# Cosine of the first four pairs of chunks from a quarter turn that TensorE adds to the phases in place

## The chip, the cores and the metric

One core of a Trainium2 chip runs the whole problem in one launch. The metric is the device time in microseconds. Five engines of the core work side by side, each through its own queue in order: TensorE (PE, matmuls into PSUM), VectorE (DVE), ScalarE (ACT, activation functions by table), GpSimd (POOL) and SyncE (SP), which here only issues DMAs. In the profile PEld is TensorE's weight load.

## The reference, cut to what matters

A gated linear recurrence with a complex decay is run over 768 steps for 4 batches and 8 heads of 48 channels; its output, with the heads put side by side (384 channels), goes through a normalised two-layer block with a residual:

```python
mag = np.sqrt(a_re * a_re + a_im * a_im)
scale = np.minimum(mag, 0.999) / (mag + 1e-06)
a_re_n, a_im_n = (a_re * scale, a_im * scale)
for t in range(S):                       # S = 768
    ar, ai = a_re_n[:, :, t, :, None], a_im_n[:, :, t, :, None]
    new_re = ar * S_re - ai * S_im
    new_im = ar * S_im + ai * S_re
    kv = np.einsum('bhd,bhe->bhde', k[:, :, t], v[:, :, t])
    S_re, S_im = (new_re + kv, new_im)
    y[:, :, t] = np.einsum('bhd,bhde->bhe', q[:, :, t], S_re)
...
xn = (x - mu) / np.sqrt(var + 1e-06) * g_ln          # x is y, heads side by side
ch = np.maximum(xn @ w_ch1, 0.0) @ w_ch2             # 384 -> 1536 -> 384
return x + ch
```

## The kernel before, in words

The recurrence is done in chunks of 128 steps. With `l` the running sum of the logarithm of the decay's size and `phi` the running sum of its angle, a product of decays between two steps is `exp(l_t - l_s) * cos(phi_t - phi_s)`, and the cosine of a difference splits into products of cosines and sines. So each key is multiplied by `exp(-l)` and stacked as (cos, sin) copies, each query by `exp(l)` and stacked likewise, and a chunk becomes ordinary masked attention plus a carried state `G`.

Two chunks make a *pair* `P`, twelve pairs in all, three to a batch. Pair 0 is worked in two halves of four heads (`PARTS = {0: 2}`). A step's name carries the pair, the half and sometimes a part: `sin.0.1` is the sine of the second half of pair 0, `mm1.2.0.1` the first layer of pair 2, column group 0, second part. Steps numbered by chunk (`atm.5`, `x.5`, `y.5`) belong to pair 5 // 2. The steps of a pair, with the engine by the letter after the colon in the plan (P, A, V, G, S for PE, ACT, DVE, POOL, SP):

- `are`, `aim`, `q`, `k`, `vf`: loads. `ln`, `iv` (ACT): logarithm and inverse of the real part. `r`: the ratio of imaginary to real part. `r2`, `u`, `l`: half the logarithm of 1 + r², added to the first logarithm, then capped, which gives the log of the decay's size. `th` (ACT): arctangent of `r`.
- `dec` (PE, L459): running sums of `l` by triangular matmuls into PSUM; `e`, `en` (ACT, L463): exponentials of them. `dps`, `decc`: the decay over a whole pair.
- `ph` (PE, L474 and L477): running sums of the angle in turns, into PSUM, with the carry of the pair before and an offset of 192 put in by the matrix `pick`. With that offset the low 16 bits of each float are the fraction of a turn, so that a 16-bit integer view `v16` of the bank is the angle reduced to (-half, half) turn. `car` (ACT L486 or DVE L489): the carry to the next pair.
- `sin` (ACT, L502): sine of `v16`. `abs` (ACT L496 or DVE L498): its absolute value into the tile `sh`. `cos` (ACT, L505): sine of a quarter turn less `sh`.
- `ke`, `qe`, `ks`, `qs`: multiplication of keys and queries by `en`, `e`, cosine (part 0) and sine (part 1). `kT`, `qT` (PE transposes, L561) with the copies `ksT`, `qsT` out of PSUM, or a DMA transpose issued by SP (L566) in their place.
- `am` (PE, L584), `atm` (DVE, times the mask), `gm`, `G` (state), `y` (PE), `x` (copy of the chunk's output), `bn` and `rstd` (mean and variance, inverse root; POOL L670 and L672), `xtr`, `xT` (transpose).
- `mm1` (PE, L684): first layer; `relu`; `mm2` (PE, L705): second layer; `ot` (DVE L719) or `oa` and `ot` (ACT L710, POOL L717): scale by `rstd` and add `x`; `st`: store.

Beside the pairs: the two weight matrices come in by `wl.0` (`w1b`) and `wl.1` (`w2b`), DMAs that POOL issues. Before each stands a one-element copy, `gate.0` and `gate.1`, which waits for a load (`k.0.1`, `aim.1.0`) so that the weights do not go ahead of it. `wgc`, `wp.*` (PE) and nine `wc.*` (DVE, L371) fold the layer's gain and mean into `w1b`. `warm.*` are matmuls without use that fill PE while it has nothing to do. `tab.log` and `tab.trig` (L739) load ACT's table for logarithm and exponential, or for sine and arctangent.

All order is written out by hand. `PLAN` is a list of steps; `Graph.run` goes through it and emits each step on the engine and PSUM bank that stand behind its name, so each engine's queue is the plan's order cut down to that engine. Tiles turn in rings (`RINGS`), PSUM has eight banks. A step that waits holds up everything behind it on its engine. The plan opens so:

```
are.0.1:S tab.log.0:A ln.0.1:A iv.0.1:A aim.0.1:S are.0.0:S pad.ks.1:G one:G ue:G car0.1:G cmean:G pick:G
ident:G uth:V zdec:G r.0.1:G aim.0.0:S are.1.0:S ln.0.0:A iv.0.0:A r.0.0:V gln:S aim.1.0:S k.0.0:S are.3.0:S
k.0.1:S r2.0.1:A u.0.1:A pad.ks.2:G l.0.1:V ln.1.0:A r2.0.0:G gate.1:G q.0.0:S q.0.1:S warm.0:P1 warm.1:P1
```

Of the kernel before, what the change touches and what calls it, by code (L numbers as in the profile page):

```python
# [33 lines left out]
GATES = (("k", 0, 1), ("aim", 1, 0))  # L34
# [17 lines left out]
warm.60:P4 warm.61:P4 ph.1.0:P2 k.1.1:S qe.0.1.0:V cos.0.1:A qs.0.1.0:V cos.0.0:A dec.0.0:P1 sin.0.0:A0
aim.3.0:S vf.1.1:S k.1.0:S abs.1.0:V2 car.1.0:V2 vf.1.0:S q.1.1:S ks.0.1.0:G pad.qs.1:G mask:G tab.log.1:A
en.0.0:A1 e.0.0:A1 qs.0.1.1:V ke.0.0.0:V qe.0.0.0:V ks.0.0.0:V ks.0.0.1:V warm.62:P5 warm.63:P5 warm.64:P5
warm.65:P5 warm.66:P5 warm.67:P5 warm.68:P5 warm.69:P5 warm.70:P5 warm.71:P5 warm.72:P5 warm.73:P5
warm.74:P5 warm.75:P5 warm.76:P5 warm.77:P5 warm.78:P5 warm.79:P5 warm.80:P5 warm.81:P5 warm.82:P5 kT.1:P4
k.2.0:S wl.0:G qs.0.0.1:V u.1.0:A ln.2.0:A qs.0.0.0:V dps.0:P5 k.2.1:S iv.2.0:A l.1.0:V kT.0:P6 qT.1:P7
tab.trig.1:A cos.1.0:A v.0:A ksT.0:V6 r.2.0:G ksT.1:V4 decc.0:V5 wgc:V qsT.1:V7 qT.0:P0 gm.0:P1 dec.1.0:P4
am.1:P6 th.2.0:A sin.1.0:A2 tab.log.2:A e.1.0:A4 r2.2.0:G u.2.0:A pad.qs.2:G qsT.0:V0 am.0:P2 G.0:V1
atm.1:V6 atm.0:V2 y.1:P0 y.0:P6 ln.3.0:A iv.3.0:A wp.2:P7 qe.1.0.0:G x.0:A6 l.2.0:V dec.2.0:P2 wl.1:G  # L60
en.1.0:A4 wp.0:P6 e.2.0:A2 x.1:A0 wc.2.0:V7 wc.2.2:V7 en.2.0:A2 are.4.0:S xtr.0:P0 wc.2.1:V7 dps.1:P7
xtr.1:P4 r.3.0:G xT.0:A0 wp.1:P5 decc.1:A7 ph.2.0:P2 wc.0.0:V6 wc.0.1:V6 bn.0:V wc.0.2:V6 r2.3.0:A xT.1:A4
wc.1.2:V5 wc.1.1:V5 wc.1.0:V5 ke.1.0.0:G ke.1.0.1:G ks.1.0.0:G v.1:G qe.1.0.1:G mm1.0.2.1:P6 gm.1:P1 G.1:V1
# [24 lines left out]
k.6.0:S qsT.9:S relu.3.1:V2 qe.5.0.1:V qs.5.0.0:V rstd.3:G q.6.1:S aim.8.0:S st.5:S mm1.3.2.0:P6 qT.8:P5
mm1.3.2.1:P6 ln.7.0:A gm.9:P1 relu.3.2:A6 vf.5.0:S mm2.7.0:P4 dec.6.0:P2 qs.5.0.1:G qsT.8:V5 mm2.7.1:P4
# [112 lines left out]
def kernel(  # L202
# [568 lines left out]
```

## Time and profile before

| | us |
|---|---|
| median of five runs | 197.81 (196.57 to 198.13) |
| the profiled execution, its own time | 196.92 |
| its span, first to last instruction | 195.0 |
| first `mm1` matmul starts | 37.70 |
| last `mm2` group starts | 187.25, and 24 matmuls follow each other |
| last `ot` | 191.35, 0.62 long |

The granted TensorE clock was 1.00 in every stage. The page gives busy time, share and count of instructions of each engine; a group line gives source line, engine, operation, what it writes and reads, how often, busy us and mean ns. In the stage table each line is a stretch of 10 us with the busy us of PE, PEld, DVE, ACT and POOL, then clock, share of the DMA engines, and GB/s. The chain of waits is followed back from the last instruction and shows, piece by piece, start, length and the work that the rest waited for.

### The profile page before, as it was taken

How to read it: one execution, taken by the hardware profiler on the slowest of the kernel's cores; microseconds unless marked ns; L12 is line 12 of the kernel's file. 1: busy time of each engine (PE TensorE's matmuls, PEld its weight loads, DVE VectorE, ACT ScalarE, POOL GpSimd, SP SyncE). 2: the span in 40 equal slices, each digit the busy share in tenths (PEclk: the TensorE clock that was granted, in tenths of full speed). 3: DMA queues.
4: the chain of work that ended last, by engine and by line, in shares of the span. 5: the costliest groups of instructions: out<-in, count | busy, mean ns of one | idle time of the engine just before them, and what ended most of it. 6: DMA issues, size and time to landing. Idle time of an engine off the chain costs nothing.

```text
span 195.0 us, 5114 instructions
## 1 busy us (share of the span) xinstructions
PE 174.1 (89%) x2031; PEld 133.4 (68%) x2032; DVE 159.9 (82%) x268; ACT 164.0 (84%) x226; POOL 108.2 (55%) x127
## 2 busy tenths in 40 slices
PE   4987455899999999999999997999999999899992
PEld 3775433577687676697887785786877758687771
DVE  1459999999999999999998799699969969835702
ACT  4799995999899999999999998997979989465160
POOL 8545558715939258045949699234981486430230
PEclk9999999999999999999999999999999999999999
DMA  5999999999998399899799989998998999992322
GB/s 150 241 237 257 175 243 179 186 243 181 227 262 190 78 187 250 202 250 241 143 237 215 218 136 285 174 221 210 256 200 152 155 197 123 266 212 88 113 84 82
DMA packets 132936, 37.76 MB, mean 194 GB/s; under 512 B 127920, under 2 KB 132528, under 8 KB 132912
## 3 DMA queue, kind: packets, MB, share of 16 engines
q1 hardware_dynamic: 130960, 35.07, 85.8%
q0 software_dynamic: 1952, 2.36, 7.5%
q8 instruction: 16, 0.26, 0.5%
q14 instruction: 8, 0.07, 0.1%
HBM read 28.31 MB, written 4.72 MB: 169 GB/s over the span
## 4 chain that ended last, share of the span: by engine, by line
PE 43%; DVE 22%; DMA 11%; ACT 10%; issue 6%; SPq 4%; POOL 2%; DVEq 0%; POOLq 0%
PE banks L705 16%; PE banks L684 12%; DMA are<-in_a_re_dram 4%; DVE atm L280 4%; SPq L566 3%; DVE w1b L371 3%; DVE l L449 3%; DMA qsT<-qs 2%; DVE h L697 2%; PE banks L584 2%; PE banks L561 2%; DMA out_dram<-ot 2%; DMA q<-in_q_dram 2%; ACT L739 2%; PE banks L459 2%
## 5 line engine op out<-in xcount | busy, mean ns | idle before, releaser
L705 PE MATMUL banks<-w2b,h 128*128 128x384 bf16 x288 | 55.5, 326 | 1.2 <-DVE atm L280 1.1
L684 PE MATMUL banks<-xT,w1b 128*128 128x256 bf16 x432 | 52.4, 272 | 0.7 <-ACT xT L275 0.4
L684 PEld LDWEIGHTS <-w1b 128*128 128x128 bf16 x432 | 41.3, 98 | 7.6 <-issue 1.7
L705 PEld LDWEIGHTS <-h 128*128 128x128 bf16 x288 | 26.2, 97 | 14.9 <-issue 1.6
L280 DVE TENSOR_TENSOR atm<-banks,mask 128x1024 bf16<-128x1024 f32 x24 | 28.9, 1216 | 4.5 <-PE banks L584 4.2
L695 ACT ACTIVATE h<-banks 128x1024 bf16<-128x1024 f32 x27 | 27.0, 1022 | 5.1 <-PE banks L684 4.9
L739 ACT ACT_TABLE_LOAD x20 | 25.7, 1283 | 1.1 <-PEq L755 0.8
L280 POOL TENSOR_TENSOR ks<-ke,trig 128x768 bf16<-128x768 bf16 (+1 forms) x11 | 17.9, 1634 | 12.3 <-DVE ke L280 7.4
L280 POOL TENSOR_TENSOR qe<-q,e 128x384 bf16<-128x384 f32 x16 | 15.9, 1003 | 13.5 <-ACT e L463 10.1
L280 POOL TENSOR_TENSOR r<-aim,are 128x768 f16<-128x768 f32 (+1 forms) x9 | 16.7, 1854 | 10.6 <-ACT are L433 10.6
L280 POOL TENSOR_TENSOR ke<-k,en 128x384 bf16<-128x384 f32 x17 | 17.1, 1012 | 8.2 <-ACT en L463 8.1
L719 DVE SCALAR_TENSOR_TENSOR ot<-banks,rstd,x 128x384 f32<-128x384 f32 x20 | 12.0, 609 | 8.4 <-PE banks L705 6.0
L584 PE MATMUL banks<-qsT,ksT 128*128 128x128 bf16 x192 | 14.6, 219 | 2.2 <-DVE qsT L277 1.6
L584 PEld LDWEIGHTS <-ksT 128*128 128x128 bf16 x192 | 12.2, 98 | 4.6 <-issue 3.0
L734 PE MATMUL banks<-u_e 128*128 128x256 f16 x83 | 11.9, 310 | 2.8 <-POOL u_e L312 2.8
L670 POOL TENSOR_SCALAR rstd<-mv 128x2 f32<-128x2 f32 x12 | 2.8, 236 | 19.8 <-DVE mv L648 19.1
L634 PE MATMUL banks<-v,atm 128*128 128x48 bf16 x192 | 11.9, 183 | 2.1 <-DVE atm L280 2.0
L449 DVE SCALAR_TENSOR_TENSOR l<-r,w 128x768 f16<-128x768 f16 (+1 forms) x13 | 12.9, 990 | 0.9 <-ACT r L445 0.8
L647 DVE BATCH_NORM_STATS2 stats<-x 128x6 f32<-128x384 bf16 x24 | 13.2, 548 | 0.3 <-ACT x L275 0.3
L634 PEld LDWEIGHTS <-atm 128*128 128x128 bf16 x192 | 10.5, 96 | 4.2 <-DVE atm L280 3.2
L280 DVE TENSOR_TENSOR qs<-qe,trig 128x768 bf16<-128x768 bf16 (+1 forms) x21 | 12.1, 597 | 1.1 <-POOL qe L280 0.8
L431 ACT ACTIVATE w<-are 128x768 f32<-128x768 f32 (+1 forms) x13 | 10.3, 793 | 2.8 <-DMA are<-in_a_re_dram 2.8
(91 smaller groups left out, 379.0 us busy)
## 6 DMA issues: line engine op xcount, KB each, us to landing
k<-in_k_dram SPq DMA_DIRECT2D x24, 192.0 KB, 3.8
q<-in_q_dram SPq DMA_DIRECT2D x24, 192.0 KB, 4.1
vf<-in_v_dram SPq DMA_DIRECT2D x24, 192.0 KB, 4.1
out_dram<-ot SPq DMA_DIRECT2D x24, 192.0 KB, 3.3
are<-in_a_re_dram SPq DMA_DIRECT2D x11, 384.0 KB, 4.8
aim<-in_a_im_dram SPq DMA_DIRECT2D x11, 384.0 KB, 5.4
w1b<-in_moe_w_ch_dram POOLq DMA_DIRECT2D x1, 1152.0 KB, 9.6
w2b<-in_moe_w_ch_dram POOLq DMA_DIRECT2D x1, 1152.0 KB, 12.9
```

Of the source, the lines that this page charges most:

```text
L280: {"DVE": nc.vector, "POOL": nc.gpsimd}[eng(name)].tensor_tensor(**kw)
L431: add(f"ln.{X}", lambda S_=S_: act(out=S_("w"), in_=S_("are"), func=AF.Ln), needs=[f"are.{X}"], uses=[("are", P), ("w", P)])
L449: nc.vector.scalar_tensor_tensor(out=S_("l"), in0=S_("r2"), scalar=0.5, in1=S_("w"), op0=ALU.mult, op1=ALU.add)
L584: nc.tensor.matmul(ps[:, h], lhsT=T("ksT", n)[:, h], rhs=T("qsT", n)[:, h], start=True, stop=True)
L634: nc.tensor.matmul(ps[:, h], lhsT=T("atm", n)[:, h], rhs=T("v", P)[:, c, h], start=True, stop=nfirst)
L647: nc.vector.bn_stats(out=T("stats", n), in_=T("x", n))
L684: nc.tensor.matmul(ps[:, jj], lhsT=w1b[:, dc, ts(gi * JG + jj, C)], rhs=T("xT", P)[:, dc].rearrange("p c t -> p (c t)"), start=(dc == 0), ...
L695: act(out=dst, in_=src, func=AF.Relu)
L705: nc.tensor.matmul(bank(f"o.{n}")[:, 0:DM], lhsT=T("h", P)[:, j, ts(c, C)], rhs=w2b[:, j], start=(j == 0), stop=(j == NJ - 1))
L719: nc.vector.scalar_tensor_tensor(out=T("ot", n), in0=bank(f"o.{n}")[:, 0:DM], scalar=T("rstd", P)[:, ds(c, 1)], in1=T("x", n), op0=ALU.mul ...
L734: g.add(f"warm.{i}", lambda i=i: nc.tensor.matmul(bank(f"warm.{i}")[:, 0:256], lhsT=u_e[:, 0, 0], rhs=u_e[:, 1].rearrange("p j t -> p (j t ...
L739: g.add(f"tab.{nm}.{i}", lambda tab=tab: nc.scalar.preload_act_table_set(tab))
```

## The change

For pairs 0 to 3 the `abs` steps are gone. After `sin` and `car` have read the phases, PE adds 0.25 (a quarter turn) to the same PSUM bank by one-row matmuls (`qt`, with the row of `pick` that holds ones), and `cos` is a second sine of the same view. Pairs 4 to 11 keep `abs`. Because `qt` adds to a bank that is already summed, `ph` sets its start flag once for a bank.

With it come: `rstd` may run on ACT, as a logarithm and an exponential (eight of twelve do); `wgc` may run on ACT and does; the cap of `l` is a step of its own, `lc`; both gates are gone, so that `wl.0` and `wl.1` go out where they stand in POOL's order; and the plan is a new one throughout. 142 steps change their engine and nearly all their place. The number of steps by engine that differ most (before, after): `ot` on DVE 20, 14 and on POOL 4, 10; `oa` on ACT 4, 10; `relu` on ACT 27, 24 and on DVE 9, 12; `x` on ACT 17, 10 and on DVE 7, 14; `ks` on POOL 11, 7; `qs` on POOL 5, 8; table loads 20, 23; `kT` and `qT` on PE 23, 22; `warm` 83, 98. The lines of the after kernel lie further down by 4 to 24: `cos` from `qt` is L513, `relu` on ACT L719, `mm1` L708, `mm2` L729, the table loads L763.

```diff
-GATES = (("k", 0, 1), ("aim", 1, 0))
+QUARTER = {0, 1, 2, 3}
...
+    eps_b = pool.tile([C, 1], FP32, name="eps_b")
+    qrow = pool.tile([C, DM], FP16, name="qrow")
...
+    g.add("qrow", lambda: nc.gpsimd.memset(qrow[ds(HALF, 1)], 0.25))
...
-    for i, (nm, P, c) in enumerate(GATES):
-        g.add(f"gate.{i}", lambda nm=nm, P=P, c=c: nc.gpsimd.tensor_copy(
...
     g.add("wl.0", lambda: nc.gpsimd.dma_start(
-        out=w1b, in_=moe_w_ch1.rearrange("(dc p) j -> p dc j", p=C)), needs=["gate.0"])
+        out=w1b, in_=moe_w_ch1.rearrange("(dc p) j -> p dc j", p=C)))
...
                     nc.tensor.matmul(ps[:, c], lhsT=pick[rows], rhs=T("car", P)[rows, fs],
-                                     start=True, stop=False)
+                                     start=(c == 0 or NS == 1), stop=False,
+                                     skip_group_check=True)
...
+            if P in QUARTER:
+                def f_qt(X=X, view=view):
+                    ps = view(f"ph.{X}")
+                    for c in range(R):
+                        nc.tensor.matmul(ps[:, c], lhsT=pick[ds(HALF, 1)], rhs=qrow[ds(HALF, 1), 0:W],
+                                         start=False, stop=True, skip_group_check=True)
+                add(f"qt.{X}", f_qt, needs=[f"ph.{X}", f"sin.{X}", "qrow"]
+                    + ([] if last else [f"car.{X}"]), ps=(f"ph.{X}", nb))
+                add(f"cos.{X}", lambda fs=fs, v16=v16: act(
+                    out=T("trig", P)[:, 0, :, fs], in_=v16(), func=AF.Sin, scale=TWO_PI_SAFE / TURN),
+                    needs=[f"qt.{X}"], uses=[("trig", P)], ps=(f"ph.{X}", nb))
+            else:
...
+            if eng(f"rstd.{P}") == "ACT":
+                act(out=t, in_=T("mv", P)[:, :, 1], func=AF.Ln, bias=eps_b)
+                act(out=t, in_=t, func=AF.Exp, scale=-0.5)
+                return
```

The new plan opens so (the `warm` steps that follow are left out):

```
are.0.0:S tab.log.0:A ln.0.0:A iv.0.0:A are.0.1:S one:G ln.0.1:A iv.0.1:A are.1.0:S aim.0.1:S car0.1:G
pad.qs.2:G aim.0.0:S k.0.0:S aim.1.0:S are.2.0:S q.0.0:S k.1.0:S aim.2.0:S zdec:G mask:G gln:S q.0.1:S
pad.ks.1:G ident:G pick:G ue:G car0.0:G pad.qs.0:G uth:V k.0.1:S vf.0.1:S pad.ks.0:G r.0.0:V ln.1.0:A
iv.1.0:A tab.trig.0:A th.0.0:A r.0.1:G th.0.1:A
...
ph.0.1:P0 vf.0.0:S r2.0.0:G r2.0.1:V r.1.0:V cmean:G r2.1.0:V
are.3.0:S q.1.1:S k.1.1:S aim.3.0:S tab.log.1:A u.0.0:A l.0.0:V lc.0.0:V car.0.1:A0 u.0.1:A u.1.0:A l.0.1:V
...
ln.2.0:A e.0.1:A1 iv.2.0:A dec.0.0:P2 e.0.0:A2
...
dps.0:P3 en.0.0:A2 en.0.1:A1 ph.0.0:P2 l.1.0:V lc.1.0:V r.2.0:V
k.2.0:S vf.1.0:S car.0.0:V2 tab.trig.1:A sin.0.0:A2 dec.1.0:P4 sin.0.1:A0 decc.0:A3 qrow:G
```

And where `qt` stands among PE's steps and ACT's in pairs 2 and 3:

```
mm1.0.2.0:P6 mm1.0.2.1:P6 qs.1.0.0:V qs.1.0.1:V relu.0.2:A6 mm1.0.0.1:P4 mm1.0.0.0:P4 relu.0.0:A4
ksT.2:A3 qt.2.0:P0 ph.3.0:P6 qe.2.0.0:V car.3.0:V6 cos.2.0:A0 l.3.0:V mm1.0.1.0:P4 mm1.0.1.1:P4 qT.3:P2
qT.2:P3 sin.3.0:A6 qsT.3:V2 qsT.2:V3 relu.0.1:A4 gm.2:P0 qt.3.0:P6 am.3:P4 G.2:A0 lc.3.0:V cos.3.0:A6
```

## The prediction

> **What bounds the kernel now.** I read the page first, then the stage table, then the chain of waits in order of time. The page:
>
> ```profile
> span 195.0 us, 5114 instructions
> PE 174.1 (89%) x2031; PEld 133.4 (68%) x2032; DVE 159.9 (82%) x268; ACT 164.0 (84%) x226; POOL 108.2 (55%) x127
> PE 43%; DVE 22%; DMA 11%; ACT 10%; issue 6%; SPq 4%; POOL 2%; DVEq 0%; POOLq 0%
> L739 ACT ACT_TABLE_LOAD x20 | 25.7, 1283 | 1.1 <-PEq L755 0.8
> ```
>
> Three engines are above 80%, so the share says little; the stages say more (columns: stage, then busy us of PE, PEld, DVE, ACT, POOL):
>
> ```profile
> 20.00:30.00 10.00, 5.31 (x92) 4.14 (x92) 9.87 (x19) 9.88 (x12) 6.08 (x5) 1.00 1.08 214
> 30.00:40.00 10.00, 7.06 (x73) 4.44 (x75) 9.93 (x16) 7.62 (x14) 7.47 (x6) 1.00 1.21 183
> 60.00:70.00 10.00, 9.46 (x119) 6.88 (x118) 9.80 (x16) 9.81 (x17) 5.68 (x5) 1.00 0.59 117
> 90.00:100.00 10.00, 10.00 (x137) 8.05 (x136) 9.97 (x17) 9.92 (x15) 7.56 (x6) 1.00 0.92 205
> 140.00:150.00 10.00, 10.00 (x133) 7.71 (x131) 7.87 (x16) 8.56 (x13) 6.01 (x6) 1.00 0.88 184
> ```
>
> From 20 to 100 us DVE and ACT are full; afterwards PE alone is. The chain of waits (start, length, what) agrees, and gives PE's pace when nothing delays it:
>
> ```profile
> 36.80 2.63 DVE w1b L371 x4
> ...
> 80.41 1.30 PE banks L705 x8
> ...
> 82.36 0.65 PE banks L459 x4
> ...
> 84.03 1.31 PE banks L684 x12
> ...
> 90.14 0.45 PE banks L584 x8
> ...
> 90.75 0.33 PE banks L477 x2
> ```
>
> So `mm2` costs PE 0.163 us a matmul, `mm1` 0.109, a transpose or an `am` product 0.056, a 384-column f16 matmul 0.163. Summed over the plan, without the fillers called `warm`, PE has 156.9 us of work. I call time minus PE work done so far the lag. From the starts in the timeline: the first `mm1` starts at 37.7 with 11.3 done (lag 26.4); `mm1.0.0.0` at 40.9 (26.8, after `w1b` on DVE); `mm1.3.0.0` at 81.6 (30.4); `mm1.4.0.0` at 100.1 (30.9); `mm1.8.0.0` at 148.1 (32.5); the last `mm2` ends at about 191.2 (34.3), and 3.8 us of `ot` and store follow. Hence 195.0 = 156.9 + 34.3 + 3.8. The profiled run took 196.92, so 1.9 lies around the span; the median of the five runs, 197.81, is 0.9 above it.
>
> **Part 1, the quarter turn.** Five `abs` go: on ACT 0.49 + 2 x 0.81 (L496), on DVE 0.56 + 0.95 (L498). Five `cos` read PSUM instead of `sh`: priced like `sin` (L502, 806 against 932; half size 484 against 604), 0.6 less. Together ACT -2.7, DVE -1.5. Added are ten `qt` matmuls of one row and 384 or 192 columns. No such shape is in the trace; the nearest is L474 (96 rows, 384 columns, 327 ns alone, 0.163 in a row), the floor 0.056 of a transpose. I take the pace of L474: 1.3 us; ends 0.6 and 2.8. Each `qt` also makes PE wait for `sin` and `car`. Behind `qt.1.0` on PE stand `y.1` and the `wp` products, which wait for `atm.1` (30 us) anyhow; behind `qt.2.0` stand `ph.3.0` and `mm1.0.1`; behind `qt.3.0` stand `am.3` and `mm2.0.0`. I walk `sin.2.0` to its end at 40.4 and `mm1.0.0.0` to 40, so no stall, and `sin.3.0` to 44.9 where PE is free at 44; if that cover is gone each costs up to 1 us.
>
> **Part 2, the new order moves work between engines.** Count of steps times the mean of the row (ns: `relu` 1022 on ACT, 1212 on DVE; `x` 478, 551; `G` 484, 548; copies of `ksT`/`qsT` 1025, 683; `ot` 609 on DVE, 915 on POOL; `qs` and `ks` 1940 and 1706 on POOL, about 600 on DVE; `r2` 844 on ACT, 1468 on POOL; `rstd` 947). ACT: abs and cos -2.7; three other abs moved, net +0.8; three more table loads 3 x 1.283 = +3.9; eight `rstd` from POOL, two tiny activations each, nearest rows 0.16 (48x8 copy) and 0.48 (128x384), taken at 0.2 by size, +3.2 (2.6 to 7.7); six `oa` (586 ns) +3.5; `qsT` and `ksT` copies +2.0; `wgc` +0.8 and `v` +0.8; less three `relu` -3.1, seven `x` -3.4, `r2` -1.3, `G`, `xT` and `decc` -2.3. Sum +2.2. DVE: abs -2.5; `relu` +3.6, `x` +3.9, `G` +1.6, `ks` and `qs` +0.6, `xT` and `decc` +1.0; `ot` -3.7, `ksT` and `qsT` -2.0, `wgc` and `v` -1.4. Sum +1.1. POOL: `ot` +5.5, `qs` +5.8, `r2` +2.9, `ks` -6.8, `rstd` -7.6, gates -0.4. Sum -0.6. PE: `qt` +1.3, transposes -0.3, sum +1.0, so 157.9. Nothing is saved in sum; what can change the time is when the work is due. DMA transposes stay 27.
>
> The Trainium skill ("ScalarE: Activation LUTs", section on table sets) says to batch activations by set, which speaks against 23 loads instead of 20. Its terms price a load at about 2.7 us; by that the three loads would be 8.1, but the rows here show 1283 ns twenty times. The same page ("What ACT_TABLE_LOAD costs") puts an activation with a pointer bias at 280 ns and one without at 186 ns plus 0.833 ns an element; by that eight `rstd` are an estimated 3.8, which no run here shows yet.
>
> **Part 3, the opening (0 to 41 us).** Today half 1 of pair 0 gets its decay first and its angles after; now the angles of both halves come first (trig table), then the decays. I walk it by the rows of today's opening. SP issues the loads 0.5 us apart and they arrive at some 200 KB a us, so `are.0.0` is there at 3.4 as now, `are.1.0` at 5.1, `aim.0.1` and `aim.0.0` at 6 to 7. POOL's constants in their new order put `u_e` at 5.9 (today 2.7), `uth` on DVE at 6.6, `r.0.0` at 7.6; POOL's `r.0.1` at 8.3. ACT: `ln`/`iv` of both halves and of pair 1 to 7.2, table to 8.45, `th.0.0` and `th.0.1` to 9.4, table to 10.7, then `u` three times, `car.0.1` and `ln.2` to 13.8, `e.0.1` (its `dec` is done at 13.6), `iv.2`, `e.0.0`, both `en` to 16.3, table to 17.6, two `sin` to 18.4, `decc`, `cos.0.0` at 19.2, `th.1`, `cos.0.1` at 20.5. DVE, which waited for `cos.0.0`, needs eight halves of `ks`, `qs`, `qe` and `r2` after it, and the last `ks` of pair 0 is ready at 22.1. Today it is ready at 20.6: 1.5 later.
>
> From there DVE waits for `u.2` (table to 21.8, `ln.3`, then `u.2` to 23.5) and runs `l.2` to 24.4, three of the four copies and `G` to 26.9, the last to 27.5, two `ke` to 28.5, `lc.2`, `atm.1` to 30.2, `atm.0`, `G`, three `wc` to 33.9, `x.0`, three `wc` to 36.4, `xT.0` to 36.8. (`lc`, split off from `l`, took 0.36 to 1.85 in its present place, longest beside a POOL operation; I take 0.6.) ACT goes from `u.2` through `e.1`, `car`, `en.1`, `iv.3`, `wgc`, table, `sin.1`, two `th`, `r2.3`, `cos.1`, `x.1` at 32.9, table, `en.2`, `e.2`, `u.3`, `decc` to `xT.1` at 37.4. So `mm1` starts at 37.5, today 37.7, but with 13.1 of PE work behind it instead of 11.3: lag 24.4. All six `wc` that `mm1.0.2` and `mm1.0.0` need are done by then, so what is lost today between 37.7 and 40.9 (26.4 to 26.8) is not lost. Opening: 24.4 against 26.8, -2.4; ends -4 and +1.5, since a walk over forty steps can miss by some 2 to 3 us.
>
> `gate.0` and `gate.1` go; `wl.0` now leaves POOL at 18.5 behind `v.0` (17.8 today), lands 9.6 later at 28, and is needed at 30.5. `wl.1` stands behind two `ks` on POOL and leaves at 34.1 (28.8 today); with its 12.9 it lands at 47.0, where PE, at lag 24.4 with 21.6 done, would want it at 46.0. Behind `mm2.0.0` on PE wait `y.2` and the next `mm1`. That costs 0 to 1.5; I take 0, since ACT sets the pace there and PE would only wait earlier for what it waits for anyway.
>
> **Part 4, 41 to 100 us.** I summed rows along both plans and compared at equal PE work done:
>
> | PE work done | ACT before, after | DVE before, after |
> |---|---|---|
> | 36 | 61.7, 61.6 | 58.8, 52.3 |
> | 52 | 81.4, 80.2 | 73.9, 67.8 |
> | 64 | 95.9, 95.2 | 88.7, 82.8 |
> | 80 | 110.5, 114.1 | 105.5, 101.0 |
> | 120 | 150.8, 158.0 | 141.3, 139.3 |
>
> DVE is 4 to 6 lighter where both are full, ACT even. The lag grows by 4.1 here today. It can't shrink by more than ACT's idle time in 40 to 100, 1.2 us in the stage table: -1.2; ends -4.1 (ACT work not needed so early) and +2.2 (the whole ACT surplus).
>
> **Part 5, 100 us to the end.** PE-bound, +3.4 of lag today. No term; ends -1.5 and +3. After the last `x` 9.3 of PE work remains instead of 11.6, so a late DMA transpose is covered less. Last stage: `bn.23` and `rstd.11` move behind `relu`, under 3.9 us of `mm2`.
>
> **Sum.** PE work +1.0, opening -2.4, part 4 -1.2: -2.6, so 194.3 for the profiled run, 195.2 against the median.
>
> **Rivals.** *ACT becomes the bound, slower.* At `mm1.8.1.1` (PE work 120) ACT has 7.2 us more behind it, 6.6 in time since successive activations overlap (164 busy for 177 summed). ACT idles 11.9 us up to 150 today, 3.6 of it in the first 10. If the new order leaves more than 5.3 of idle by then (11.9 less 6.6), it is late; half way, with 9 idle, the price is 3.7, less the 1.4 left of the opening: +2.3, 200.1. For: ACT is 98% busy from 40 to 110. Against: some of the surplus is work ahead of need. Chance 0.40. *PE takes it back, no change.* The opening comes as walked, -2.4, PE work +1.0, the late `w2b` +1.0, DVE's relief unused because ACT is full: -0.4, 197.4. Chance 0.13. That five `abs` vanish is certain from the code. The forecast, faster, has 0.47, its own range 192 to 196.8.
>
> **Range.** Below: the opening at its -4 (1.6 more) and part 4 half way to its -4.1 (1.5 more): -5.7, 192.1, taken as 192.0. Above: the first rival, which with the walk's error of 2 spreads over 198.1 to 202.1; up to 201.0 some quarter of it is left out, one in ten. 0.5% (1.0 us) is about what a measurement of this kernel can tell from no change.
>
> **What would show it.** First `mm1` at 37.5 with two `wc` groups done; lag at `mm1.3.0.0` below 29.5; table loads 23; DVE idle in 40 to 100 instead of 1.1 some 4. Wrong: first `mm1` after 39, a wait of L729 on `w2b`, or PE waiting for ACT's `relu` or `en` around 145 to 155.

## The result and the profile after

The changed kernel takes 199.99 us (median of 22 runs) beside 197.84 us of the kernel before (43 runs): ratio 1.0076, 95% interval [1.0056, 1.0096], slower by 0.56 to 0.96%. Its runs scatter more, 197.5 to 204 against 196.6 to 198.9 without one outlier each; the ratios leave disturbed runs out (13 of the 22 stay, with a median of 199.46 us), while the profiles of e3, e6 and e9 to e12 below are of such runs, so that a loss that only these profiles show is not taken as the kernel's. The profiled run took 198.72 us, 1.3 under the median; its span is 197.0 us, that of before 195.0.

The page (of the last two lines the first is the chain's shares by engine, the second the group of table loads):

```profile
span 197.0 us, 5157 instructions
...
PE 177.2 (90%) x2051; PEld 134.7 (68%) x2052; DVE 161.3 (82%) x270; ACT 166.9 (85%) x237; POOL 106.1 (54%) x118
...
PE 37%; ACT 25%; DVE 16%; SPq 9%; DMA 6%; issue 5%; POOL 1%; DVEq 0%; POOLq 0%; ACTq 0%
...
L763 ACT ACT_TABLE_LOAD x23 | 29.5, 1283 | 1.2 <-PEq L779 0.8
```

ACT has 2.9 us more, DVE 1.4 more, POOL 2.1 less. On the chain ACT went from 10 to 25%. The stages:

```profile
20.00:30.00 10.00, 8.26 (x102) 6.79 (x101) 9.28 (x22) 9.91 (x16) 1.50 (x3) 1.00 1.00 190
30.00:40.00 10.00, 6.98 (x85) 4.40 (x86) 7.89 (x12) 8.65 (x14) 8.68 (x8) 1.00 1.00 210
...
60.00:70.00 10.00, 9.82 (x128) 7.07 (x126) 9.49 (x20) 9.60 (x15) 4.72 (x5) 1.00 1.08 224
...
90.00:100.00 10.00, 9.26 (x105) 6.53 (x105) 9.59 (x15) 9.80 (x17) 6.41 (x6) 1.00 0.76 162
...
130.00:140.00 10.00, 9.57 (x130) 6.69 (x128) 8.25 (x12) 9.89 (x19) 7.34 (x6) 1.00 1.01 227
```

From 20 to 40 us DVE is no longer full (17.2 of 20, before 19.8); whether by the quarter turn or by the new order, these rows don't tell. POOL is almost empty from 20 to 30 and then busy for 8.7 of 10. From 90 to 100 PE now has holes, and ACT is full from 130 to 140 (9.89, before 8.86).

The lag (time minus PE work done) shows where the 2.0 us of span come from:

| until | lag before | lag after | change of the difference |
|---|---|---|---|
| `mm1.0.0.0` (41 us) | 26.8 | 26.7 | -0.1 |
| `mm2.5.2` (80) | 30.0 | 29.2 | -0.8 |
| `mm2.8.2` (110) | 30.9 | 32.9 | +2.8 |
| `mm1.6.0.0` (126) | 32.3 | 32.9 | -1.4 |
| `mm2.13.2` (137) | 32.4 | 34.0 | +1.0 |
| last `mm2` | 34.3 | 35.3 | -0.6 |

The differences add to +1.0 (before rounding), and PE's work is 1.0 more: +2.0, which is the difference of the spans. So three things are to be explained: an opening that gained nothing, a loss of 2.8 from 80 to 110 us, and 1.0 from 131 to 139.

**The opening.** POOL in the changed kernel (start, length, what; in brackets the idle time before):

```profile
20.95 0.55 POOL L348 MEMSET qs<- 128x512 bf16 x1
30.52 1.81 POOL L284 TENSOR_TENSOR r<-aim,are 128x768 f16<-128x768 f32 x1 [9.02 <-ACT trig L502]
32.29 1.64 POOL L284 TENSOR_TENSOR ks<-ke,trig 128x768 bf16<-128x768 bf16 x1
34.71 1.64 POOL L284 TENSOR_TENSOR ks<-ke,trig 128x768 bf16<-128x768 bf16 x1 [0.79 <-ACT trig L513]
36.29 1.08 POOL L354 DMA_DIRECT2D w2b<-in_moe_w_ch_dram  x1
```

POOL stands still for 9.0 us before `r.3.0`. The row names ACT's `sin.1.0`, but the chain of waits names the load of `aim.3.0`, issued at 19.05 and 11.2 us under way, and ACT in its turn waits for `r.3.0`:

```profile
19.05 11.22 DMA aim<-in_a_im_dram
...
32.36 0.84 ACT L473 ACTIVATE th<-r 128x768 f16<-128x768 f16 x1 [1.28 <-POOL r L284]
```

Behind `th.3.0` on ACT waits `cos.1.0`. Behind `r.3.0` on POOL wait the two `ks.1.0`, one of them for `cos.1.0` too, and then the issue of `w2b`, which leaves at 36.29 instead of the 34.1 that I walked to, and with its 12.9 us lands at 49.2. `mm2.0.0` starts at 49.23.

**80 to 110 us.** DVE, then one row of POOL and PE's longest wait there:

```profile
98.59 0.55 DVE L284 TENSOR_TENSOR ks<-ke,trig 128x768 bf16<-128x768 bf16 x1
99.06 1.99 DVE L284 TENSOR_TENSOR ke<-k,en 128x384 bf16<-128x384 f32 x1
101.18 1.03 DVE L284 TENSOR_TENSOR ks<-ke,trig 128x768 bf16<-128x768 bf16 x2
102.13 0.68 DVE L281 COPY ksT<-banks 128x1024 bf16<-128x1024 bf16 x1
```

```profile
98.94 1.69 POOL L284 TENSOR_TENSOR qs<-qe,trig 128x768 bf16<-128x768 bf16 x1 [2.35 <-issue]
...
102.86 0.81 PE L465 MATMUL banks<-l,u_e 128*128 128x384 f16 x4 [1.09 <-DVE ksT L281]
```

`ke.6.0.1`, 0.55 us elsewhere, took 1.99 beside POOL's `qs.6.0.1` (98.94 to 100.63), which had begun 0.12 us before it; it ended 0.42 us after that. PE's transposes for `ksT.11` were done by 99.8, their copy came at 102.1, and PE stood. Besides this 1.1 us PE waited 0.6 us for ACT's `car.6.0` and 0.4 for DVE's `atm.6` there; in the kernel before its longest wait from 80 to 110 us is 0.3.

### The profile page after: what moved, and what is told of

Same layout as the page of the kernel before. It is cut to its first block, busy times and chain, and to the rows that moved or that the text cites. A ratio compares the mean times of both kernels' runs of the same rounds, so it can differ in the third digit from the quotient of the medians.

```text
span 197.0 us, 5157 instructions
## 1 busy us (share of the span) xinstructions
PE 177.2 (90%) x2051; PEld 134.7 (68%) x2052; DVE 161.3 (82%) x270; ACT 166.9 (85%) x237; POOL 106.1 (54%) x118
## 4 chain that ended last, share of the span: by engine, by line
PE 37%; ACT 25%; DVE 16%; SPq 9%; DMA 6%; issue 5%; POOL 1%; DVEq 0%; POOLq 0%; ACTq 0%
PE banks L708 14%; PE banks L729 12%; DMA aim<-in_a_im_dram 6%; SPq L392 5%; ACT h L719 5%; ACT L763 4%; SPq L433 4%; PE banks L604 3%; DVE atm L284 2%; ACT e L469 2%; DVE h L721 2%; DVE l L457 2%; ACT en L469 2%; PE banks L465 1%; DVE l L454 1%
## 5 line engine op out<-in xcount | busy, mean ns | idle before, releaser
L729 PE MATMUL banks<-w2b,h 128*128 128x384 bf16 x288 | 53.6, 326 | 0.0
L708 PE MATMUL banks<-xT,w1b 128*128 128x256 bf16 x432 | 52.7, 272 | 0.4
L708 PEld LDWEIGHTS <-w1b 128*128 128x128 bf16 x432 | 41.0, 98 | 6.9 <-issue 1.0
L729 PEld LDWEIGHTS <-h 128*128 128x128 bf16 x288 | 26.1, 97 | 13.7 <-issue 0.2
L763 ACT ACT_TABLE_LOAD x23 | 29.5, 1283 | 1.2 <-PEq L779 0.8
L719 ACT ACTIVATE h<-banks 128x1024 bf16<-128x1024 f32 x24 | 24.1, 1026 | 7.3 <-PE banks L708 7.2
L284 POOL TENSOR_TENSOR ke<-k,en 128x384 bf16<-128x384 f32 x16 | 15.3, 965 | 14.0 <-ACT en L469 11.0
L758 PE MATMUL banks<-u_e 128*128 128x256 f16 x98 | 13.5, 297 | 5.6 <-POOL u_e L318 5.6
L721 DVE TENSOR_SCALAR h<-banks 128x1024 bf16<-128x1024 f32 x12 | 14.5, 1217 | 3.7 <-PE banks L708 3.5
L284 POOL TENSOR_TENSOR qs<-qe,trig 128x768 bf16<-128x768 bf16 x8 | 13.6, 1711 | 3.6 <-issue 2.3
L758 PEld LDWEIGHTS <-u_e 128*128 128x128 f16 x98 | 10.3, 107 | 7.7 <-POOL u_e L318 5.3
L741 POOL TENSOR_TENSOR ot<-ot,x 128x384 f32<-128x384 f32 x10 | 9.2, 915 | 11.3 <-ACT ot L734 11.3
L284 POOL TENSOR_TENSOR ks<-ke,trig 128x768 bf16<-128x768 bf16 x7 | 12.6, 1802 | 4.5 <-ACT trig L513 4.3
L454 DVE SCALAR_TENSOR_TENSOR l<-r,w 128x768 f16<-128x768 f16 (+1 forms) x13 | 12.9, 989 | 2.0 <-ACT r L450 1.8
L654 PEld LDWEIGHTS <-atm 128*128 128x128 bf16 x192 | 10.8, 96 | 3.7 <-DVE atm L284 1.6
L284 DVE TENSOR_TENSOR ks<-ke,trig 128x768 bf16<-128x768 bf16 (+1 forms) x19 | 11.7, 623 | 2.0 <-ACT trig L502 1.1
## 6 DMA issues: line engine op xcount, KB each, us to landing
w2b<-in_moe_w_ch_dram POOLq DMA_DIRECT2D x1, 1152.0 KB, 12.9
```

Of the source, the lines that this page charges most:

```text
L284: {"DVE": nc.vector, "POOL": nc.gpsimd}[eng(name)].tensor_tensor(**kw)
L454: nc.vector.scalar_tensor_tensor(out=S_("l"), in0=S_("r2"), scalar=0.5, in1=S_("w"), op0=ALU.mult, op1=ALU.add)
L654: nc.tensor.matmul(ps[:, h], lhsT=T("atm", n)[:, h], rhs=T("v", P)[:, c, h], start=True, stop=nfirst)
L708: nc.tensor.matmul(ps[:, jj], lhsT=w1b[:, dc, ts(gi * JG + jj, C)], rhs=T("xT", P)[:, dc].rearrange("p c t -> p (c t)"), start=(dc == 0), ...
L719: act(out=dst, in_=src, func=AF.Relu)
L721: nc.vector.tensor_scalar(out=dst, in0=src, scalar1=0.0, scalar2=None, op0=ALU.max)
```

## The experiments

All are timed against the kernel before on the same chip; e5 to e8 ran together, and e5 is the changed kernel once more:

> The changed kernel itself, unaltered, so that the other kernels of this batch can be read against it on the same chip. Span 197.0 us or a little more; lag of mm1.0.0.0 26.7, of mm1.4.1.0 32.9, of mm2.13.2 34.0, end 35.3.

It measured 200.37 us, and its lag ends at 36.4 instead of 35.3: two profiles of one kernel differ by up to 1.1 us, so a smaller difference between single profiles shows nothing by itself. The lag of each profiled run (us; "clock" where the profile shows less than full clock from 20 to 60 us):

| kernel | ratio [95%] | `mm1.0.0.0` | `mm2.0.0` | `mm2.5.2` | `mm1.4.1.0` | `mm1.6.1.0` | `mm2.13.2` | end |
|---|---|---|---|---|---|---|---|---|
| before | | 26.8 | 26.8 | 30.0 | 30.7 | 32.3 | 32.4 | 34.3 |
| changed | 1.0076 | 26.7 | 27.6 | 29.2 | 32.9 | 33.0 | 34.0 | 35.3 |
| e5, changed again | 1.0108 [1.0068, 1.0148] | 26.3 | 28.1 | 29.4 | 33.8 | 34.1 | 35.1 | 36.4 |
| e1 | 1.0150 [1.0107, 1.0193] | 24.4 clock | 25.0 | 32.7 | 33.4 | 35.0 | 35.1 | 36.6 |
| e2 | 1.0229 [1.0173, 1.0285] | 28.8 clock | 31.3 | 33.7 | 37.6 | 39.1 | 40.0 | 41.4 |
| e3 | 1.0043 [1.0003, 1.0084] | 24.4 | 26.5 | 28.2 | 31.6 | 31.8 | 34.8 | 37.1 |
| e4 | 1.0158 [1.0106, 1.0210] | 26.1 | 26.9 | 28.6 | 34.2 | 34.4 | 35.5 | 36.8 |
| e6 | 1.0088 [1.0053, 1.0124] | 26.2 clock | 30.1 | 31.7 | 35.6 | 37.1 | 38.1 | 39.4 |
| e7 | 1.0052 [1.0027, 1.0078] | 26.7 clock | 27.8 | 29.4 | 32.5 | 33.2 | 34.2 | 35.5 |
| e8 | 1.0193 [1.0153, 1.0233] | 29.1 clock | 29.4 | 32.1 | 38.0 | 38.2 | 38.9 | 40.0 |
| e9 | 1.0078 [1.0045, 1.0111] | 25.0 | 25.7 | 28.7 | 33.1 | 33.3 | 36.5 | 38.9 |
| e10 | 1.0112 [1.0065, 1.0160] | 25.3 | 26.0 | 28.3 | 31.0 | 32.8 | 37.1 | 39.4 |
| e11 | 1.0165 [1.0114, 1.0216] | 26.9 clock | 30.8 | 32.4 | 35.5 | 36.8 | 38.0 | 40.3 |
| e15 | 1.0035 [0.9998, 1.0073] | 26.2 | 26.9 | 28.5 | 31.7 | 32.3 | 33.4 | 34.7 |
| e16 | 1.0202 [1.0155, 1.0249] | 26.0 | 28.2 | 29.2 | 33.7 | 35.2 | 35.6 | 39.6 |
| e17 | 1.0132 [1.0095, 1.0169] | 26.8 clock | 27.5 | 29.1 | 31.4 | 32.1 | 32.7 | 36.4 |
| e18 | 1.0104 [1.0066, 1.0142] | 24.0 | 26.2 | 27.9 | 30.8 | 31.6 | 32.4 | 35.9 |

Read the rows from left to right: what a kernel gains or loses between two columns.

**Is it the quarter turn?** `e1_quarter_alone` puts it into the kernel before, `e2_no_quarter` takes it out of the changed one:

```
e1 (old order):  -abs.1.0:V2 -cos.1.0:A   +sin.1.0:A2 ... qt.1.0:P2 ... cos.1.0:A2   (likewise pairs 0, 2, 3)
e2 (new order):  -qt.1.0:P6 -cos.1.0:A6   +abs.1.0:V6 ... cos.1.0:A                  (likewise pairs 0, 2, 3)
```

> The kernel before with the quarter turn alone: abs of pairs 0 to 3 goes, sin and car come first, qt and the second sine take their places, everything else of the old plan stays. Two theories. Theory order: the quarter turn itself is about neutral, the loss of the changed kernel comes from the rest of its new plan; PE work +1.3 us against ACT -2.7 and DVE -1.5 in a stage that DVE and ACT fill, so a span of 194.3 to 195.8 us and a ratio to before of 0.996 to 1.004. Theory quarter turn: the ten matmuls and PE's waits for sin are the loss; a span of 196.3 to 197.3 and a ratio of 1.007 to 1.012.

> The changed kernel with the quarter turn undone: abs stands where qt stood, on the engines of before (DVE for 0.0 and 1.0, ACT for the others), cosine from abs; the rest of the new plan stays. Theory order: the loss stays, span 196.5 to 198 us (PE -1.3, but ACT +2.7 and DVE +1.5 in the full stage), ratio 1.004 to 1.013. Theory quarter turn: the loss goes, span 195 to 195.8, ratio 1.000 to 1.003.

Measured: e1 200.52 us, e2 202.16. Both ratios lie above the ranges of both theories. In the old order the opening comes at lag 24.4, 2.4 earlier than before; then it climbs by 7 between 45 and 73 us. From 39 to 48 us ACT stands twice for PE's `qt` (L505 of e1), 5.8 us in all:

```profile
40.46 0.81 ACT L509 ACTIVATE trig<-banks 128x768 bf16<-128x768 int16 x1 [1.13 <-PE banks L505]
...
48.18 0.81 ACT L509 ACTIVATE trig<-banks 128x768 bf16<-128x768 int16 x1 [4.66 <-PE banks L505]
```

The second row is `cos.3.0`: its `qt.3.0` stands on PE behind `am.2`, which started at 47.1 and had waited for DVE's copy of `qsT`. A load of `q` issued at 28.55 was 11.6 us under way too. ACT's `iv.4.0` comes only after this, and POOL's `r` waited 3.7 us for it. In the changed kernel ACT never waits for `qt`. So the quarter turn brings a wait that neither theory had, of ACT's queue for PE's, and what it costs depends on where `qt` stands. In the new order taking the quarter turn out costs 1.2 to 1.5% (1.0229 against the changed kernel's 1.0108 and 1.0076), 2.4 to 3 us, although in e2's profile `aim.3.0` landed early, at 23.3. There the quarter turn is a gain, and the new order without it is 2.3% slower than the kernel before.

**The opening's load.** `e3_th3_later` takes pair 3's `r` and `th` out of the way; `e9_loads` makes the load early instead:

```
e3:  POOL  -r.3.0 behind wl.0            +r.3.0 behind wl.1
     ACT   -th.3.0 r2.3.0 behind th.2.0  +r2.3.0 u.3.0 behind v.1, th.3.0 behind tab.trig.3
e9:  SP    are.3.0 [+aim.3.0] q.1.1 k.1.1 [-aim.3.0] ... aim.4.0 [-are.5.0 -aim.5.0] ... k.3.1 [+are.5.0 +aim.5.0]
```

> The changed kernel with r.3.0 moved behind wl.1 on POOL and th.3.0, r2.3.0 and u.3.0 moved behind v.1 on ACT, so that neither engine stands waiting for the load of aim.3.0, which lands at 30.3 us. Theory order: POOL's two ks of pair 1 start at 30.4 instead of 32.3, ACT no longer idles 1.3 us at 31 to 32.4, the first mm1 starts at 38.2 to 38.8 instead of 39.1, wl.1 leaves at 34 to 35 instead of 36.3 and mm2.0.0 starts 1 to 2 us earlier than 49.2; span 195.6 to 196.5, 0.5 to 1.4 less than the changed kernel. Theory quarter turn: the opening is covered later, span 196.8 to 197.2.

> The changed kernel with three loads moved on SP's queue alone: aim.3.0 two places up, right behind are.3.0 and so ahead of w1b's load on POOL's queue, and are.5.0 and aim.5.0 behind k.3.1, and so out of the way of w2b's load. Theory (the quarter turn freed ACT and DVE in the opening, and the loads then set its end: aim.3.0, issued at 19.05 beside w1b, landed at 30.3 and held r.3.0 on POOL, th.3.0 on ACT and the ks.1.0 behind r.3.0; w2b, issued at 36.3 beside four 384 KB loads, landed at 49.2 as mm2.0.0 began): aim.3.0 lands by 25, lag 24.4 to 25 at mm1.0.0.0 instead of 26.3 to 26.7, w2b lands by 47.5 and mm2.0.0's lag is 25 to 26 instead of 27.6 to 28.1; the end 1 to 2 us lower. Rival (the DMA engines are full from 0 to 60 us, so that another load lands late instead): the lag at mm2.0.0 is 27.5 or more, and the time within 0.5 us of the changed kernel's.

Measured: e3 199.21 us, e9 199.88. (The first `mm1` of the changed kernel is at 39.7, not at the 39.1 of e3's expectation.) POOL in e9:

```profile
27.08 1.81 POOL L282 TENSOR_TENSOR r<-aim,are 128x768 f16<-128x768 f32 x1 [6.40 <-DVE qsT L279]
30.35 1.64 POOL L282 TENSOR_TENSOR ks<-ke,trig 128x768 bf16<-128x768 bf16 x1 [1.45 <-DVE ke L282]
32.96 1.64 POOL L282 TENSOR_TENSOR ks<-ke,trig 128x768 bf16<-128x768 bf16 x1 [0.97 <-ACT trig L511]
34.53 1.08 POOL L352 DMA_DIRECT2D w2b<-in_moe_w_ch_dram  x1
```

Issued at 16.5, ahead of `w1b`, the load took 5.8 us instead of 11.2. `r.3.0` runs 3.4 us earlier, `w2b` leaves 1.8 earlier, and `mm2.0.0` has lag 25.7 instead of 27.6 and 28.1. e3 reaches 24.4, the very value of my walk, and e18, with the same moves, 24.0. So the opening's 2.4 us were there and were lost to `r.3.0` and `th.3.0` standing ahead of `ks.1.0` and `cos.1.0`. The earlier load alone does less: e15 and e17, which have it too, begin at 26.2 and 26.8. By time e9 is the changed kernel again (1.0078), and e3 (1.0043) is under it by less than the intervals can tell. So what came early does not reach the end. In e9's profile 3.2 us go between `mm1.6.1.0` and `mm2.13.2`, but that run took 202.36 us, and in e14, which is e9 with fewer stores, only 1.1 go there: where e9 loses it is not shown.

**80 to 110 us.** `e4_ke6_pool` moves the stretched operation to POOL, `e7_ksT11` moves the late copy ahead of it:

```
e4:  -ke.6.0.1:V   +ke.6.0.1:G behind ke.6.0.0
e7:  mm1.4.0.0 [+kT.11 +bn.8:V +ksT.11:V] ke.6.0.1:V ks.6.0.0:V [-kT.11] ks.6.0.1:V ... [-ksT.11 -bn.8]
```

> The changed kernel with one step, ke.6.0.1, on POOL directly behind ke.6.0.0 instead of on DVE, where it took 1.99 us at 99.1 instead of some 0.55. Theory order (DVE steps lengthened beside POOL hold PE at 101 to 103): DVE's chain between 96 and 102 is 1.4 to 2 us shorter, PE's lag at mm1.4.1.0 falls from 32.9 to 31 to 31.9, and 0.3 to 1.5 us of it is left at the end. Theory quarter turn: the end is the same within 0.2 us.

> The changed kernel with DVE's copy ksT.11 (and the statistics bn.8) ahead of ke.6.0.1, ks.6.0.0 and ks.6.0.1. Theory (PE stood 1.09 us before dec.7.0 because ksT.11 waited on DVE behind ke.6.0.1, which POOL's qs.6.0.1 stretched to 1.99 us): the wait goes, lag at mm1.4.1.0 31.8 instead of 32.9, and the time falls by 0.5 to 1.1 us. Rival (DVE is full there and the next of its products is late instead): lag at mm2.11.2 is 32.9 again and the time is the changed kernel's within 0.3 us.

e4 missed: 200.67 us. With more on POOL other operations of DVE were stretched (`ks.5.0.1` 1.99 us, `l.7.0` 1.66), and `mm2.7.2` came at lag 34.2 instead of 31.6. e7 holds against e5, on the same chip: 199.33 us beside 200.37. DVE in e7:

```profile
100.53 0.18 DVE L666 BATCH_NORM_AGGREGATE mv<-stats 128x2 f32<-128x6 f32 x1
100.80 0.69 DVE L279 COPY ksT<-banks 128x1024 bf16<-128x1024 bf16 x1
101.41 0.56 DVE L282 TENSOR_TENSOR ke<-k,en 128x384 bf16<-128x384 f32 x1
102.07 1.03 DVE L282 TENSOR_TENSOR ks<-ke,trig 128x768 bf16<-128x768 bf16 x2
```

The copy is 1.3 us earlier, `ke.6.0.1` is back at 0.56, and at `mm1.4.1.0` the lag is 1.3 lower than in e5, 0.9 at the end. Against the first profile of the changed kernel it is 0.4 lower there and 0.2 higher at the end, and at `mm2.11.2` it is 33.1, near the rival's 32.9. The ratios (1.0052 against 1.0108 and 1.0076) put the edit's worth at 1.1 and 0.5 us, the second within the noise. So the single wait and its cause are shown; its share of the 2.8 us is 0.5 to 1.1.

**Is ACT the bound from 120 to 155?** `e8_rstd_pool` gives eight `rstd` back to POOL (and drops the 23rd table load); `e16_ln11` changes ACT's order where the lag rose from 131 to 139:

```
e8:   -rstd.{0,1,2,3,6,7,10,11}:A -tab.log.11   +the same :G
e16:  ACT  [-ln.11.0 -rstd.6 -iv.11.0] en.9.0 e.9.0 x.15 [+ln.11.0 +rstd.6 +iv.11.0]
```

> The changed kernel with all twelve rstd on POOL, as in the kernel before, and so without the 23rd table load; ACT loses 8 times some 0.5 us and 1.28 us. Theory that ACT is the bound from 119 to 140 us: lag at mm2.13.2 33.3 instead of 34.0 and the end 1 us lower, time 198 or less. Rival that ACT is only one of three equal bounds: POOL's two instructions beside DVE's products, and the wait of ot for them, cost as much, and the time is the changed kernel's within 0.5 us.

> The changed kernel with ACT's ln.11.0, rstd.6 and iv.11.0 behind x.15, and nothing else. Theory (from 131 to 139 us ACT's two logarithm steps of pair 11 and rstd.6, which wait for the load are.11.0 landing at 134.5 to 137, stand ahead of en.9, e.9 and x.15, and PE's transposes of x.15 wait for them): the lag rises by 0.3 or less from mm1.6.1.0 to mm2.13.2, instead of 1.0 here and up to 3.2 in kernels that come there earlier; end 0.7 to 1.0 us lower. Rival (DVE's chain of atm.14, atm.15 and x.14 is as late as ACT's): the lag rises by 0.8 or more, and the time is the changed kernel's within 0.3 us.

e8 missed: 202.58 us, 0.8% slower than e5 by the ratios. ACT fell to 163.0 us busy and the lag rises 0.7 from `mm1.6.1.0` to `mm2.13.2` instead of 1.0, but 5.9 from `mm2.5.2` to `mm1.4.1.0` instead of e5's 4.4. The work takes more of POOL (113.2 us busy, 7.1 more) than it frees of ACT (3.9); that this makes the kernel slower is likely but not shown, since the opening of this profile was late too (29.1). e16 is right on its spot and wrong on the time, 201.96 us. The lag rises there by 0.4 instead of 1.0, and then (the chain of waits, and below it what PE waited for from 128 to 160 us: total, times, longest):

```profile
138.64 0.80 ACT e L467
139.44 0.37 ACT x L277
139.81 0.74 ACT w L434
...
140.97 0.73 ACT are L436
...
142.99 0.38 ACT xT L277
```

```profile
PE banks L706 <- ACT xT L277: 1.6, 1, 1.6
PE banks L706 <- DVE xT L279: 1.3, 1, 1.3
```

`x.15` comes early, `xT.14` behind `ln.11` and `iv.11` late, and PE waits 1.6 us there and 1.3 for DVE's `xT` before `mm1.8`. Steps moved within ACT's queue here only changed which product was late.

**Does the DMA volume set the pace?** `e12_slim_changed`, `e13_slim_before` and `e14_slim_loads` store only one row of 128 of tiles 0 to 15, in the changed kernel, the kernel before and e9 (all else is computed):

```
+            m = 1 if n < 16 else C
-                out=...[:, pp * R + c], in_=T("ot", n)),
+                out=...[0:m, pp * R + c], in_=T("ot", n)[0:m]),
```

> The changed kernel, but of the outputs of tiles 0 to 15 only one row of 128 is stored (3.1 of some 11 MB less for the DMA engines; the queue's order, all compute and all buffers as they are). Theory that the loads and transposes on SP's queue set the pace from 100 to 160 us, and that the changed kernel loses there what it has gained: end lag at least 1.5 us under the changed kernel's 35.3 to 36.4, time under 198. Rival that the engines alone set it (ACT 19.8 of 20 us busy from 120 to 140, DVE 19.3 of 20 from 80 to 120): time within 0.7 us of the changed kernel's.

> The kernel before, with the same stores cut. Theory that DMA is what tells the two apart: gains clearly less than the changed kernel does from the same cut, 0 to 1 us (ratio 0.995 to 1.0), so that the two slim kernels lie within 1 us of each other. Rival that both are bound by DMA alike: gains as much as the changed kernel does.

> e9_loads with the same stores cut. Theory (the opening's 2 us are given back only because the transposes and loads around 125 to 140 us do not come earlier): the jump of 3.2 us between mm1.6.1.0 and mm2.13.2 is 1 us or less, and it ends 1.5 to 2.5 us under e12_slim_changed. Rival (given back to the engines): ends within 0.7 us of e12_slim_changed.

Measured against the whole kernel before: e13 0.9944 [0.9920, 0.9967], e12 1.0194 [1.0148, 1.0241], e14 1.0160 [1.0118, 1.0201]. The profile of e12 has 34.8 MB moved, that of the changed kernel 37.9 (not the "some 11" of the expectation). Less traffic helps the old kernel by half a per cent and does not help the changed one, so my theory for 100 to 160 us falls. On the loads of the opening these runs say nothing, since the first store is issued after 50 us; that `aim.3.0` is late by its place in the queue rests on e9. Why e12 is slower than the changed kernel (1.0108 and 1.0076) isn't settled: in its profile `aim.3.0` was issued at 20.67 instead of 19.05, at a clock of 0.92, and the opening's lag was 30.3. What e12 leaves out cannot have made that late opening; whether its other runs had it too is not known.

**Do the edits add up?** `e6_load_and_th3` is e3 with `th.3.0` behind `sin.2.0` and `are.11.0` ahead of four transposes on SP; `e10_loads_ksT11` is e9 with e7's edit and this `are.11.0`; `e11_all` adds e3's; `e15_aim3_ksT11` is `aim.3.0` early and e7; `e17_three_edits` is e15 and e16; `e18_th3_three` is e3, e7 and e16.

> The changed kernel with pair 3's r on POOL behind w2b's load, its th on ACT behind sin.2.0, its u and r2 behind v.1, and the load are.11.0 on SP ahead of four transposes. Theory (the opening's 2.4 us were lost to th.3.0 waiting for a load that landed at 30.3; the later loss of the earlier trial of this order came from ln.11.0 waiting on ACT for are.11.0, issued at 130.0 and landed at 135.2): lag 24.4 at mm1.0.0.0, about 25.5 at mm2.0.0, 31.0 to 31.6 at mm1.6.0.0, no wait of ACT for a DMA near 133, end about 33.5 and the time 1.5 to 2 us under the changed kernel's. Rival (whatever is gained early is given back because ACT, DVE and PE are all full from 40 to 140): the lag ends at 35.3 as in the changed kernel, time within 0.5 us of it.

> The loads' order of e9_loads, the order of DVE at ksT.11 of e7_ksT11, and are.11.0 on SP ahead of four transposes. Theory that these are separate losses that add: the lag falls by 1.5 to 2 us in the opening and by 1.0 at mm1.4.1.0, end at 32.5 to 33.5, time 196.5 to 197.5, at or under the kernel before. Rival that later stages full on ACT, DVE and PE eat what comes early: end lag above 34.5, time as e7_ksT11 (ratio 1.005).

> As e10_loads_ksT11, and r.3.0 behind w2b's load on POOL, u.3.0 and r2.3.0 behind v.1, th.3.0 behind the table load of pair 3 (e3_th3_later). Theory: with aim.3.0 early the reordering of pair 3 has nothing left to save, time within 0.5 us of e10_loads_ksT11. Rival (r.3.0 and th.3.0 held ks.1.0 and sin.1.0 back by their own durations, 1.8 us on POOL and 0.8 on ACT, whenever the load lands): lag at mm1.0.0.0 0.5 to 1.5 us under e10_loads_ksT11, and the time too.

> The changed kernel with aim.3.0 two places up on SP and ksT.11 ahead of ke.6.0.1 on DVE, and nothing else: the two single edits that gained most by themselves, without the later are.5.0 that held ln.5.0 at 53 us in e9_loads. Theory: lag 25.0 to 25.5 at mm1.0.0.0, 31.0 to 31.5 at mm1.4.1.0, time 198 or less, within 0.5% of the kernel before. Rival: what comes early at 131 us is given back by 140, time 199 to 200.

> The changed kernel with aim.3.0 two places up on SP, ksT.11 ahead of ke.6.0.1 on DVE, and ln.11.0, rstd.6 and iv.11.0 behind x.15 on ACT. Theory that the three losses are separate: lag 25 to 26 at mm1.0.0.0, 31 to 31.7 at mm1.4.1.0, 31.5 to 32.5 at mm2.13.2, time 196.5 to 198, at or under the kernel before. Rival that full engines give it back: time 198.5 or more.

> As e17_three_edits, but with e3_th3_later's order of pair 3 in place of the earlier aim.3.0. Theory: lag 24.4 to 26 at mm1.0.0.0, the loss of 3.0 us that e3_th3_later had from 130 to 139 us falls to 1 or less, time 196 to 198. Rival as in e17_three_edits.

They don't. e18 is the clearest: its lag is 0.7 to 2.7 us under the changed kernel's from the first `mm1` to `mm2.13.2` (there 32.4 against 34.0), as the three causes promise, and its end is 0.6 above it (35.9 against 35.3), because PE waits 1.1 us at `mm1.7` for ACT's `xT` and 1.3 at `mm1.8` for DVE's. e17 has the same two waits, 1.3 us each. In the profiles of e6, e10 and e11 the gain goes elsewhere, or does not come (e6 and e11 begin at 26.2 and 26.9); in that of e10 a transposed `ksT`, 4.9 us under way, kept PE waiting 2.4 us near 133, at a clock of 0.91. The best kernels found are e15 (198.15 us in its profiled run), e3 and e7; none beats the kernel before, and e15 can't be told from it.

## Why the prediction was wrong

The direction was wrong. The time (199.99) lies in the range 192 to 201 and 0.1 from the price of the first rival, 200.1; that it is so near is luck, as the last point says.

- **Part 1, right.** No wait beyond the bounds: PE's idle time before the ten `qt` sums to 1.3 us, and the wide ones last as long as their 96-row neighbour (323 against 326 ns). In e3 and e18, which open earlier, PE waits 1.1 us more, for `sin.2.0` before `qt.2.0`: the "up to 1 us" of a lost cover. The part asked what PE waits for at `qt`, not what ACT then waits for; that wait is nothing in the changed kernel, but 5.8 us in e1. Price by e2, in the new order: a gain of 2.4 to 3 us.
- **Part 2, near in sum.** ACT +2.9 (predicted +2.2), DVE +1.4 (+1.1), POOL -2.1 (-0.6). `rstd` took 291 and 203 ns, eight of them 4.0 us where I had 3.2; the estimate from the Trainium skill ("ScalarE: Activation LUTs", "What ACT_TABLE_LOAD costs"), 3.8, was nearer. All 23 table loads took 1283 ns as before. PE's +1.0 closes the sum of the spans.
- **Part 3, wrong: -2.4 was -0.1.** This step failed first. The walk let loads "arrive at some 200 KB a us" and of the loads after pair 1 followed only the weights; it named "two `th`" on ACT without asking when `aim.3.0` is there (it took 11.2 us), and did not put `r.3.0` on POOL in front of `ks.1.0` at all. The first `mm1` began at 39.7 instead of 37.5. e3 and e18 with those two steps out of the way reach 24.4 and 24.0. The late `w2b`, taken at 0, cost 0.1 us in the changed kernel's profile and 1.0 in e5's, inside its 0 to 1.5: `mm2.0.0` starts at 49.23 and 49.67, and the 0.65 us of `dec.3.0` ahead of it on PE start at 48.44 and 48.02.
- **Part 4, wrong: -1.2 was +2.0** by 110 us, near its upper end of +2.2. Until 80 us it came (-0.8). DVE idle from 40 to 100 is 2.5 us, up from 1.1, not 4. The table compared sums of nominal durations: it could not see the order within DVE's queue, where e7 found a wait of 1.1 us, nor that DVE's operations are stretched beside POOL's added `qs`. From 80 to 100 us the DVE operations that took over 0.1 us more than the shortest of their kind lost 3.4 us by it, before 0.6.
- **Part 5, no term, was -1.0 net,** made of two: the kernel before loses more after 110 us, and the changed one loses 1.0 from 131 to 139, mostly where PE waits for `x.14` of DVE and `x.15` of ACT. The reading that this part began with, DVE and ACT full from 20 to 100 us and then PE alone, was off in two rows of the kernel before: ACT is busy 7.62 of 10 from 30 to 40, PE 8.91 from 110 to 120.
- **Rivals.** ACT is nearly full from 120 to 155 (34.25 of 35 us busy, before 30.95), and up to 150 us it idles 9.0 us, the very half-way value that the rival's price assumed. But that ACT sets the time is not shown: the larger loss, 80 to 110, has waits for DVE in it, e8 with 3.9 us less on ACT is slower, and in e16, e17 and e18 PE waits for DVE's `xT` as well as for ACT's. So the right price is luck in part. That PE takes it back fails: the opening did not come as walked.

Of the three marks I had set as "wrong if", the first `mm1` after 39 showed. The wait on `w2b` showed in e5 (0.8 us) and hardly in the first profile; a wait of PE for ACT's `relu` or `en` from 145 to 155 did not come. What stays open: the remaining 1.7 to 2.3 us of the loss from 80 to 110, of which PE's waits for `car.6.0` and `atm.6` name 1.0 and for which no edit was tried; why the changed kernel's opening scatters so; and why no set of edits brings the kernel under the one before.

## What to carry to other kernels

When work is taken off the bounding engines, list which loads the next steps need and where each stands in its queue. `aim.3.0` landed at 28.2 before and at 30.3 here; it became the bound because what waits for it was put in front of steps that PE needs, and held up everything behind it on its engine. In a kernel with three engines full, compare queues step by step, not sums: in e16 to e18 each mended wait moved to the next product in ACT's or DVE's queue, and of the 2.7 us that e18 gained by 40 us nothing was left at 190. When a matmul is put between two activations, look also at what the second one then waits for: in e1 ACT stood 5.8 us behind PE's queue. An operation handed to the idle engine (POOL) can be paid for by the busy one (DVE) when POOL begins first, as with `ke.6.0.1`.

## What the runs showed of the hardware that was not expected

- The 384 KB load of `aim.3.0`, issued at 16.3 to 17.9 us, 1.2 us or more ahead of the 1152 KB load of `w1b` on POOL's queue, took 5.4 to 6.4 us (e2, e9, e10, e11, e15, e17); issued 0.1 to 0.9 us ahead of it, 10.8 to 11.4 (the changed kernel, e3 to e8).
- DVE operations from SBUF to SBUF are stretched beside a POOL operation, by much and not always. In the changed kernel it goes by which began first: eight `ks`, `qs`, `ke`, `qe` of DVE that began while a POOL operation ran ended 0.40 to 0.42 us after it, whatever its length, and six `lc` 0.21 to 0.22 after it. Where DVE began first or within 0.01 us of it, `ke` and `ks` took their 0.54 to 0.56 us, and at 113.45 it was POOL's `qs` that took longer, 2.05 us instead of 1.63 to 1.69. In figures: `lc` (128x768 f16) took 0.35 to 0.36 us in all three cases with POOL idle and 0.34 to 1.46 beside POOL, `ke` 0.55 and in one case 1.99. `atm`, which reads PSUM, was not: 1.19 to 1.23 in all 24 cases, 17 of them beside POOL.
- With the same opening the granted clock from 20 to 40 us differs from profile to profile: 1.00 in the changed kernel, e4, e5 and e16 (lag at `mm1.0.0.0` 26.0 to 26.7), 0.89 to 0.92 in e7, e8 and e12 (26.7, 29.1, 30.3).
